# A sequence FFT, a maxout layer and a SoLU layer on one core: the first batch's first transform in f32, its input laid out by loads, other fillers and other priorities

## The chip, the cores and the metric

The kernel runs on one core of one Trainium2 chip. The time is the device time of one execution in microseconds, from three runs of the kernel before, and one more execution that the hardware profiler recorded. TensorE (PE) multiplies matrices and loads weights beside that (PEld), VectorE (DVE), ScalarE (ACT) and GpSimd (POOL) do the rest, and SyncE (SP) issues all DMA transfers on one queue.

## The reference

```python
X = np.fft.fft(x, axis=1)                 # x: 8 batches x 3072 rows x 256, f32
X = np.fft.fft(X, axis=2)
x = X.real.reshape(8 * 3072, 256)
h = np.maximum(np.maximum(x @ w1, x @ w2), x @ w3)      # 256 -> 768
x = h @ w_out                                           # 768 -> 256
h = x @ w_in                                            # 256 -> 1024
e = np.exp(h - h.max(-1)); sm = e / (e.sum(-1) + 1e-9)
solu = h * sm
ln = (solu - mean(solu)) / sqrt(var(solu) + 1e-6) * g_ln
out = ln @ w_out2                                       # 1024 -> 256
```

## The kernel before

Products that need the accuracy of f32 are done in f16 with a high and a low part of each factor: ScalarE makes the high part (`split_hi`, L367), VectorE or GpSimd the low part (`split_lo`, L370), and TensorE adds three products (`TERMS`: high by high, high by low, low by high).

**The transforms.** The transform over the 256 columns is folded into the weights of layer 1: TensorE multiplies them with a table of cosines (cw) in f32 (L996, L1003, L1101). The transform over 3072 rows has two steps. A batch of x is loaded in four chunks c (`x_load`, L409, tile xs); VectorE (batch 0) or GpSimd (the others) folds each with its mirror image (L416, L458, tile uv). The sum of squares over the batch gives a scale, a power of two (L425 to L441, tile xb). x is split into f16 parts with that scale (`x_hi`, `x_lo`, tile uh: in batch 0 straight from uv by L367 and L370). **alpha** (`alpha_mm`, L496, L499) multiplies it with the table cal; ScalarE casts the high part out (L527, tile x) and VectorE the low part (L531). `last_mm` does one row that stands alone. SP transposes the result (tile z), and **beta** (L555, table cb) is the second step; its parts are pq.

**The layers.** A batch gives 6 blocks of 512 rows, 48 in all. In each block layer 1 (L660, tile l, weights wl and w3l; L681, L701 and L702 put the two halves of a product together in sv, L707 takes the maximum), its second product (m, L726, tile rhl as input), then h (L790), the SoLU and the norm on VectorE, ScalarE and GpSimd, and the last product (omm, L865) follow each other. TensorE does 12 groups of l, 6 of m, 4 of h and 4 of omm in a block.

**The weights** arrive as 64-bit numbers. `from_f64` loads the two words (L951, tile raw), ScalarE takes the exponent (L963) and VectorE puts an f32 together with three instructions (L967, L968, L970). The raw words of w_out and w_out2 share the buffers xs and uv with x. Subtraction (L990), folding, a bound of the largest element (am, spread, L390), a scale (sc) and the split into wl, wo, win, w3l and wf follow, all before or between the first blocks.

**The order.** The program is written by a list scheduler in Python (`Schedule`). Each operation has an engine, a duration, a due time `vt` (in blocks) plus a number from the table `BIAS`, dependences and buffers that it takes and gives back (`CAPACITY`). On each engine the ready operation with the earliest start, and among those with the smallest due time, comes next. So `BIAS` sets the order of instructions on every engine. Where the plan leaves TensorE idle before the first h, `keep_warm` puts matmuls of zeros (L1315, tile spare from zz) into the gap.

Of the kernel before, what the change touches and what calls it, by code (L numbers as in the profile page):

```python
# [1361 lines left out]
```

## Time and profile before

| | us |
|---|---|
| median of 3 runs | 1998.37 (1997.97 to 1999.53) |
| profiled execution | 2002.85 |
| its span, first to last instruction | 2001.1 |
| TensorE busy in the span | 1975.3 |
| VectorE busy in the span | 1696.1 |

The granted TensorE clock is 0.997 of full speed in the mean. A row of the timeline or of the costliest groups names the line, the engine, the operation, and the output and inputs by their names in the program; a bracket gives the idle time of the engine ahead of it and what ended it. An f32 matmul leaves two records in the trace, so 16 records of such a line are 8 matmuls. In the profiled execution layer 1 starts at 78 us and h at 118 us after the first instruction. What comes before is loading, decoding and folding weights and batch 0's transforms.

### The profile page before, as it was taken

The numbers are of one execution on the slowest core, as the hardware profiler recorded it, in microseconds if no ns is written. First come the engines' busy times: TensorE is split into PE (matmuls) and PEld (weight loads), VectorE is DVE, ScalarE is ACT, GpSimd is POOL, SyncE is SP. The second block draws the span as 40 slices with busy tenths as digits, with TensorE's granted clock in tenths as the row PEclk, the third lists the DMA queues.
The fourth block names the chain that finished last, engine by engine and source line by source line (L and its number), as shares of the span: only waits on it lengthen the run. The fifth ranks groups of instructions, "written<-read, shape, count | busy, mean of one in ns | idle before, by whom it ended". The sixth has DMA issues, their size and how long they took to land.

```text
span 2001.1 us, 40923 instructions
## 1 busy us (share of the span) xinstructions
PE 1975.3 (99%) x15041; PEld 1348.0 (67%) x15041; DVE 1696.1 (85%) x3886; ACT 1493.0 (75%) x2929; POOL 1315.2 (66%) x1395
## 2 busy tenths in 40 slices
PE   8899999999999999999999999999999999999998
PEld 4556666766666666766677666666667666666666
DVE  7888889888888888888888888888888888888885
ACT  5778888876787677877778767787677766776775
POOL 0389997955588556976569656765556665655653
PEclk9999999999999999999999999999999999999999
DMA  8424754633444334443434444333343333333334
GB/s 282 96 51 103 136 119 78 130 80 70 85 89 113 72 82 75 110 91 76 80 75 106 80 80 80 65 75 80 70 85 70 76 73 75 75 76 63 75 78 103
DMA packets 471819, 178.81 MB, mean 89 GB/s; under 512 B 452697, under 2 KB 452922, under 8 KB 468410
## 3 DMA queue, kind: packets, MB, share of 16 engines
q1 hardware_dynamic: 471618, 176.20, 42.1%
q8 instruction: 117, 1.92, 0.4%
q14 instruction: 84, 0.69, 0.1%
HBM read 37.75 MB, written 25.17 MB: 31 GB/s over the span
## 4 chain that ended last, share of the span: by engine, by line
PE 82%; DVE 6%; POOL 5%; ACT 3%; DMA 3%; issue 2%; SPq 0%; POOLq 0%; DVEq 0%; ACTq 0%
PE omm L865 22%; PE h L790 21%; PE l L660 19%; PE m L726 16%; PE beta L555 2%; PE alpha L496 1%; POOL uv L458 1%; DMA xs<-in_x_dram 1%; DVE l L681 1%; POOL xs L416 1%; POOL vh L851 1%; POOL rhl L716 1%; DMA vt<-vh 1%; ACT jk L825 1%; POOL mo L741 1%
## 5 line engine op out<-in xcount | busy, mean ns | idle before, releaser
L865 PE MATMUL omm<-wf,vt 128*128 128x256 f16 x4608 | 533.4, 273 | 2.8 <-ACT ob L872 1.7
L790 PE MATMUL h<-win,mo 128*128 128x512 f16 x2280 | 523.4, 379 | 1.6 <-DVE v L820 1.3
L716 POOL TENSOR_TENSOR rhl<-sv,rhl 128x512 f16<-128x512 f32 x288 | 334.4, 1162 | 269.5 <-ACT rhl L711 255.6
L865 PEld LDWEIGHTS <-vt 128*128 128x128 f16 x4608 | 450.3, 98 | 75.3 <-issue 1.9
L660 PE MATMUL l<-pq,wl 128*128 128x256 f16 (+2 forms) x3456 | 445.2, 272 | 7.2 <-DVE sv L707 3.1
L851 POOL TENSOR_TENSOR vh<-v,vh 128x1024 f16<-128x1024 f32 x188 | 400.8, 2132 | 75.8 <-ACT vh L847 62.7
L681 DVE SCALAR_TENSOR_TENSOR l<-ny,wn,l 128x256 f32<-128x256 f32 (+1 forms) x672 | 317.6, 483 | 155.1 <-ACT bs L367 141.9
L726 PE MATMUL m<-rhl,wo 128*128 128x512 f16 x1728 | 414.8, 379 | 0.1
L660 PEld LDWEIGHTS <-wl 128*128 128x128 f16 x3456 | 330.9, 97 | 108.0 <-DVE sv L702 11.9
L790 PEld LDWEIGHTS <-mo 128*128 128x128 f16 x2304 | 223.6, 98 | 240.6 <-DVE v L820 4.6
L367 ACT ACTIVATE bs<-l 128x256 f32<-128x256 f32 x560 | 206.1, 380 | 153.7 <-PE l L660 120.2
L825 ACT ACTIVATE jk<-v,hst 128x1024 f16<-128x1024 f32 x192 | 220.4, 1148 | 73.5 <-DVE v L820 72.4
L799 DVE TENSOR_REDUCE hst<-h 128x1 f32<-128x1024 f32 x190 | 231.7, 1219 | 50.7 <-PE h L790 49.7
L726 PEld LDWEIGHTS <-wo 128*128 128x128 f16 x1728 | 163.9, 98 | 153.0 <-issue 0.4
L820 DVE SCALAR_TENSOR_TENSOR v<-h,hst,e 128x1024 f32<-128x1024 f32 x190 | 243.2, 1280 | 23.7 <-ACT e L814 17.5
L814 ACT ACTIVATE e<-h,hst,xb 128x1024 f32<-128x1024 f32 x190 | 228.9, 1205 | 6.3
L711 ACT CAST rhl<-sv 128x512 f16<-128x512 f32 x288 | 176.0, 613 | 73.3 <-DVE sv L707 38.4
L707 DVE SCALAR_TENSOR_TENSOR sv<-l,sv 128x512 f32<-128x512 f32 x288 | 197.8, 687 | 3.6
L847 ACT CAST vh<-v 128x1024 f16<-128x1024 f32 x192 | 199.6, 1039 | 0.9 <-DMA vt<-vh 0.9
L838 POOL TENSOR_SCALAR hst<-hst,sc 128x1 f32<-128x1 f32 x192 | 66.2, 345 | 136.3 <-ACT jk L825 111.4
L741 POOL TENSOR_TENSOR mo<-s,mw 128x512 f16<-128x512 f32 x96 | 121.0, 1276 | 27.3 <-ACT mw L367 21.8
L872 ACT ACTIVATE ob<-omm,hst 128x256 f32<-128x256 f32 x192 | 89.9, 469 | 57.6 <-PE omm L865 42.1
(167 smaller groups left out, 2323.3 us busy)
## 6 DMA issues: line engine op xcount, KB each, us to landing
xs<-in_x_dram SPq DMA_DIRECT2D x32, 768.0 KB, 6.3
out_dram<-ob SPq DMA_DIRECT2D x96, 256.0 KB, 2.2
raw<-in_w_dram SPq DMA_DIRECT2D x4, 768.0 KB
vt<-vh SPq DMA_TRANSPOSE x192, 4.3
xs<-in_w_out_dram SPq DMA_DIRECT2D x8, 256.0 KB, 6.2
raw<-in_w_in_dram SPq DMA_DIRECT2D x4, 512.0 KB, 4.0
cb<-in_c_beta_dram SPq DMA_DIRECT2D x1, 1553.0 KB, 8.8
x<-in_w_dram SPq DMA_DIRECT2D x2, 768.0 KB
```

Source lines behind the costliest of these rows:

```text
L367: act.activation(dst, src, AF.Copy, scale=scale)
L660: mm(o, w_[w], hl[:, a, e, c0:c0 + n_], start=(n == 0), stop=(n == 2))
L681: dve.scalar_tensor_tensor(p[:, 0:WA], pq[s][1][:, 0:WA], w, p[:, 0:WA], ALU.mult, ALU.add)
L716: pool.tensor_tensor(t[:, 1], svs.pop((s, j, 0)), t[:, 0], ALU.subtract)
L726: mm(m[:, h], wo[:, w, j, hs], t[:, a], start=(j == 0 and n == 0), stop=(j == NJF - 1 and n == 2))
L790: mm(hp[:, f], m[:, a, d, ts_], win[:, w, d, fs], start=(n == 0), stop=(n == 5))
L799: dve.tensor_reduce(st[:, 0], y["h"], op=ALU.max, axis=AX.XY, negate=True)
L814: act.activation(y["e"], y["h"], AF.Exp, bias=st[:, 11], scale=xbt[s // NSB][:, 12:13], accum_out=st[:, 3])
L820: dve.scalar_tensor_tensor(y["v"], y["h"], st[:, 2], y["e"], ALU.mult, ALU.mult, accum_out=st[:, 4])
L825: act.activation(new(hpool[0], "jk", [128, 2, 512], F16), y["v"], AF.Square, bias=st[:, 4], scale=-float(FF2), accum_out=st[:, 6])
L851: engine.tensor_tensor(y["vh"][:, 1], y["v"].rearrange("p a b -> p (a b)"), y["vh"][:, 0], ALU.subtract)
L865: mm(y["o"][:, 0:D], vt[:, a * 8 + c], wf[:, w, c], start=(n == 0), stop=(n == 23))
```

## The change

1. In batch 0, `x_hi` and `x_lo` are gone. Alpha multiplies uv itself, in f32, with a new f32 table calf; x's scale is put on that table by one ScalarE instruction (`cals`). 33 matmuls stand for 99, and `last_mm` has 2 for 4. The buffer uv is given back by alpha.
2. x lies in memory in the order of its loads, so that the 8 KiB of a row of a chunk, and the rows of a chunk, follow each other; before, the rows of a chunk were 32 KiB apart.
3. calf is loaded after x, cal later than before. The table of ones is gone, and the factor 1/1024 of the mean of w_out2's rows is applied where the mean is copied out of PSUM. zz has 256 columns in place of 512.
4. `keep_warm` fills a gap wholly, with matmuls of 256 columns, where it filled three quarters with matmuls of 512: 377 of them in place of 149, of which 154 in a row at the start.
5. `BIAS` has new numbers, within 60 blocks in place of some 2000, and own keys for blocks 0 to 2. The plan's durations of a few loads change.

With these the order of nearly every engine changes. On SP, cw was the first load, and now it follows the first two chunks of x.

```diff
-BIAS = {("xla", 0): -534.137, ("xgh", 0): 286.232, ("xfly", 0): -6.751, ("xsq", 0): 385.004, ("xhi", 0): 285.602,
...
+BIAS = {("xla", 0): -20.556, ("xgh", 0): 23.969, ("xfly", 0): -58.75, ("xsq", 0): -12.676, ("al", 0): 23.231, ("ah",
...
+    full = out.reshape(NA * NJ + 1, 3 * 2 * NQ * NJ) * 16.0
...
+    return table, np.ascontiguousarray(np.concatenate([full, last], axis=1).astype(np.float32))
...
+    calf = wp.tile([97, c_first.shape[1]], F32, name="calf")
...
-        sp.dma_start(t[0:96], x[b, :, c * GC:(c + 1) * GC])
+        sp.dma_start(t[0:96], x[b, c])
...
     def alpha_mm(b, c, h):
...
-        u = xuh[b, c]
+        u = xuh[b, c] if b else xuv[b, c]
...
         for g in range(GC):
             n, kind = (97, 1 + h) if c == 0 and g == 0 else (96, 0)
+            if b == 0:
+                mm(p[:, g * 96:(g + 1) * 96], u[0:n, h, g], calf[0:n, kind * 96:(kind + 1) * 96])
+                continue
             for i, (a, w) in enumerate(TERMS):
                 mm(p[:, g * 96:(g + 1) * 96], u[0:n, a, h, g], table(kind, w, n), start=(i == 0), stop=(i == 2))
-        if c == 0 and h == 1:
+        if c == 0 and h == 1 and b == 0:
+            mm(p[0:1, 0:96].rearrange("p (q j) -> p q j", j=2)[:, :, 0], u[:, 1, 0, 0:1],
+               calf[:, 96:192].rearrange("p (q j) -> p q j", j=2)[:, :, 0])
+        elif c == 0 and h == 1:
...
     def last_mm(b):
...
+            if b == 0:
+                mm(p[0:1, o:o + n], calf[:, 3 * 96:3 * 96 + 1], xuv[b, 0][:, h, 0, 0:n])
+                continue
...
-        op(("xla", *k), "SP", 3500 if b else 2600, x_load, k, v - 0.5, deps=[("xla", b, c - 1)] if c else [("xla", b - 1, NCH - 1)] * (b > 0) + [("open",), ("gd", "f", 1)] * (b == 1),
+        op(("xla", *k), "SP", 3500 if b else 2200, x_load, k, v - 0.5, deps=[("xla", b, c - 1)] if c else [("xla", b - 1, NCH - 1)] * (b > 0) + [("open",), ("gd", "f", 1)] * (b == 1),
...
+        if b == 0:
+            return
         v += 0.2
-        normed = b > 0
-        if normed:
-            op(("xnm", *k), "ACT", 1040, x_norm, k, v, deps=[("xsc", b)])
...
-                op(("al", *kh), "PE", 520, alpha_mm, kh, v + 0.04 * h, deps=[("xlo", b, c), ("cal",)] + [("al", b, 0, 0)] * (not first) + [("al", b, c, 0)] * h,
+                op(("al", *kh), "PE", 520 if b else 760, alpha_mm, kh, v + 0.04 * h,
+                   deps=[("xlo", b, c) if b else ("xfly", b, c), ("cal",) if b else ("cals",)] + [("al", b, 0, 0)] * (not first) + [("al", b, c, 0)] * h,
+    def const_load5():
+        sp.dma_start(calf[0:96], c_first[0:96])
+        sp.dma_start(calf[96:97], c_first[96:97])
...
-    zz = wp.tile([128, 512], F16, name="zz")
+    zz = wp.tile([128, 256], F16, name="zz")
...
-    ones = wp.tile([128, 128], F32, name="ones")
-    pool.memset(ones, 1.0 / FF2)
...
-    op(("cal",), "SP", 900, const_load, (), -0.85, lag=2000)
+    op(("calf",), "SP", 900, const_load5, (), -0.85, lag=2000)
+    op(("cals",), "ACT", 360, lambda: split_hi(calf, calf, xbt[0][0:97, 11:12]), (), -0.85, deps=[("calf",), ("xsc", 0)])
+    op(("cal",), "SP", 900, const_load, (), -0.25, lag=2000)
...
-        put(("ld", *key), "SP", 3.4 * n, f64_load, (key, srcs, n, home), v - 0.2, deps=after, take=[home] * first + [*take], lag=1900)
+        put(("ld", *key), "SP", 3.0 * n, f64_load, (key, srcs, n, home), v - 0.2, deps=after, take=[home] * first + [*take], lag=1900)
...
-            mm(p[:, 0:D], ones, w2_rows(c), start=(c == 0), stop=(c == 7))
+            mm(p[:, 0:D], unit, w2_rows(c), start=(c == 0), stop=(c == 7))
...
-        act.copy(mean, tmp.pop("mean")[:, 0:D])
+        split_hi(mean, tmp.pop("mean")[:, 0:D], 1.0 / FF2)
...
-        n = int(gap * 0.75 / 216)
+        n = int(gap / 109 + 0.5)
...
-            mm(p[:, 0] if tag == "h" else p, zz[:, 0:128], zz)
+            mm(p[:, 0, 0:256] if tag == "h" else p[:, 0:256], zz[:, 0:128], zz)
...
-        "x": np.stack([xs[:, n[:96]][..., X_PAIRS], xs[:, m[:96]][..., X_MIRROR]], axis=3),
+        "x": np.stack([xs[:, n[:96]][..., X_PAIRS], xs[:, m[:96]][..., X_MIRROR]], axis=3).reshape(
+            B, 96, NCH, GC, 2, D).transpose(0, 2, 1, 3, 4, 5),
```

Three places show how the order moves. The first is VectorE around the first casts of alpha. xb is x's scale, L967, L968 and L970 are the decode (of a half of w_out2 on uv, of the layer-1 weights on st), L370 on uh the low parts of x, L531 alpha's low parts. Before:

```order
L440 TENSOR_SCALAR xb<-xb 128x1
L967 TENSOR_SCALAR uv<-uv 128x1024
L441 RECIPROCAL xb<-xb 128x1
L968 SCALAR_TENSOR_TENSOR uv<-xs,uv 128x1024
L970 SCALAR_TENSOR_TENSOR uv<-xs,uv 128x1024
L370 SCALAR_TENSOR_TENSOR uh<-uv,xb,uh 97x1024
L370 SCALAR_TENSOR_TENSOR uh<-uv,xb,uh 96x1024
L531 TENSOR_TENSOR x_355<-alpha,x_355 128x6x16x4 x2
L967 TENSOR_SCALAR st<-st 128x768
L968 SCALAR_TENSOR_TENSOR st<-raw,st 128x768
```

And now, with the same lines under new numbers (L454 and L455 the scale, L989, L990 and L992 the decode, L548 alpha's low parts):

```order
L454 TENSOR_SCALAR xb<-xb 128x1
L455 RECIPROCAL xb<-xb 128x1
L989 TENSOR_SCALAR uv<-uv 128x1024
L990 SCALAR_TENSOR_TENSOR uv<-xs,uv 128x1024
L548 TENSOR_TENSOR x_452<-alpha,x_452 128x6x16x4 x2
L989 TENSOR_SCALAR st<-st 128x768
L992 SCALAR_TENSOR_TENSOR uv<-xs,uv 128x1024
L990 SCALAR_TENSOR_TENSOR st<-raw,st 128x768
L548 TENSOR_TENSOR x_452<-alpha,x_452 128x6x16x4
```

The low parts of x are gone, and alpha's low parts stand ahead of the last step of the decode on uv.

The second place is VectorE around the low parts of the layer-1 weights (wl), after their scale sc. am and spread lead to the scale of the third product's weights, et is the row that stands alone. Before:

```order
L1027 RECIPROCAL sc<-am 128x1
L1034 TENSOR_SCALAR wn<-wn,sc 128x12
L370 SCALAR_TENSOR_TENSOR wl_74<-st,sc,wl_74 128x768 x4
L531 TENSOR_TENSOR x_355<-alpha,x_355 128x6x16x4 x4
L390 TENSOR_REDUCE am<-spread 128x2
L361 TENSOR_SCALAR am<-am 128x2
L364 TENSOR_SCALAR am<-am 128x2
L1027 RECIPROCAL sc<-am 128x1 x2
```

And now:

```order
L1049 RECIPROCAL sc<-am 128x1
L1056 TENSOR_SCALAR wn<-wn,sc 128x12
L548 TENSOR_TENSOR x_452<-alpha,x_452 128x6x16x4
L535 TENSOR_TENSOR et<-last,et 1x129
L384 SCALAR_TENSOR_TENSOR wl_75<-st,sc,wl_75 128x768 x4
L989 TENSOR_SCALAR uv<-uv 128x1024
L990 SCALAR_TENSOR_TENSOR uv<-xs,uv 128x1024
L1141 TENSOR_REDUCE am<-w3f 128x1
L992 SCALAR_TENSOR_TENSOR uv<-xs,uv 128x1024
L384 SCALAR_TENSOR_TENSOR pq<-beta,pq 128x256 x2
L989 TENSOR_SCALAR st<-st 128x512
L404 TENSOR_REDUCE am<-spread 128x2
```

All of alpha's low parts of batch 0 now come ahead of wl, and the decode of the other half of w_out2 on uv stands between wl and the next scale.

The third place is TensorE at alpha's first matmuls. prep is the fold of the layer-1 weights st with cw. Before:

```order
L1003 MATMUL prep<-cw,st 128x1 x6
L1315 LDWEIGHTS zz
L1315 MATMUL spare<-zz 128x512
L996 MATMUL prep<-st,cw 128x384 x8
L496 LDWEIGHTS uh
L496 MATMUL alpha<-cal,uh 128x96
```

And now:

```order
L1018 MATMUL prep<-st,cw 128x384 x4
L504 MATMUL alpha<-calf,uv 128x96 x8
L509 MATMUL alpha<-calf,uv 1x48
L1018 MATMUL prep<-st,cw 128x384 x4
L504 MATMUL alpha<-calf,uv 128x96 x8
```

Four of the eight matmuls of this part of the fold have moved behind alpha's first nine.

## Rows read from the trace of the kernel before

**Rows 1.** The page's head and part 1: busy us, share, instructions.

```profile
span 2001.1 us, 40923 instructions
PE 1975.3 (99%) x15041; PEld 1348.0 (67%) x15041; DVE 1696.1 (85%) x3886; ACT 1493.0 (75%) x2929; POOL 1315.2 (66%) x1395
```

**Rows 2.** Stretches: length, busy us by engine, granted clock, DMA share, GB/s.

```profile
0.00:79.00 79.00, 68.74 (x388) 42.05 (x389) 60.79 (x98) 48.08 (x91) 9.17 (x16) 0.94 0.69 208
79.00:118.00 39.00, 34.48 (x237) 20.07 (x236) 34.71 (x91) 31.04 (x65) 21.90 (x17) 0.96 0.28 64
118.00:200.00 82.00, 78.39 (x594) 50.70 (x593) 71.86 (x174) 64.85 (x128) 77.47 (x70) 1.00 0.43 94
...
200.00:1900.00 1700.00, 1697.81 (x13145) 1168.81 (x13143) 1460.03 (x3381) 1282.04 (x2527) 1157.05 (x1229) 1.00 0.42 84
1900.00:2001.00 101.00, 95.85 (x687) 66.33 (x684) 68.76 (x145) 67.00 (x123) 49.58 (x66) 1.00 0.43 89
```

**Rows 3.** The same for L1315 alone (fillers; PE, PEld, clock).

```profile
0.00:200.00 200.00, 40.51 (x149) 15.31 (x149) 0.97 0.50 133
```

**Rows 4.** Timeline of PE: start, us, engine, line, operation, tiles, records.

```profile
78.11 1.76 PE L660 MATMUL l<-pq,wl 128*128 128x256 f16 x12
...
118.37 2.89 PE L790 MATMUL h<-win,mo 128*128 128x512 f16 x12
...
122.61 2.75 PE L726 MATMUL m<-rhl,wo 128*128 128x512 f16 x12
```

**Rows 5.** Timeline of DVE; the bracket is the wait ahead.

```profile
6.65 0.56 DVE L967 TENSOR_SCALAR st<-st 128x768 int32<-128x768 int32 x1 [6.65 <-ACT st L963]
...
22.57 1.22 DVE L416 TENSOR_TENSOR xs<-xs 96x1024 f32<-96x1024 f32 x1 [0.50 <-DMA xs<-in_x_dram]
...
29.45 1.22 DVE L416 TENSOR_TENSOR xs<-xs 96x1024 f32<-96x1024 f32 x1 [1.25 <-DMA xs<-in_x_dram]
...
46.72 0.56 DVE L531 TENSOR_TENSOR x<-alpha,x 128x384 f16<-128x384 f32 x1 [4.09 <-ACT x L527]
...
69.55 1.07 DVE L531 TENSOR_TENSOR x<-alpha,x 128x384 f16<-128x384 f32 x2 [0.81 <-ACT x L527]
71.42 0.42 DVE L390 TENSOR_REDUCE am<-spread 128x2 f32<-128x256 f32 x1 [0.80 <-PE spread L386]
...
76.97 0.42 DVE L370 SCALAR_TENSOR_TENSOR pq<-beta,pq 128x256 f16<-128x256 f32 x1 [1.37 <-ACT pq L367]
```

**Rows 6.** Costliest groups, first 110 us: count, busy us, mean ns, idle before.

```profile
L370 DVE SCALAR_TENSOR_TENSOR uh<-uv,xb,uh 96x1024 f16<-96x1024 f32 x3 | 3.7, 1275 | 0.0
...
L370 DVE SCALAR_TENSOR_TENSOR uh<-uv,xb,uh 97x1024 f16<-97x1024 f32 x1 | 1.3, 1277 | 0.0
```

**Rows 7.** The page's part 6, DMA issues: KB each, us to landing.

```profile
xs<-in_x_dram SPq DMA_DIRECT2D x32, 768.0 KB, 6.3
...
raw<-in_w_in_dram SPq DMA_DIRECT2D x4, 512.0 KB, 4.0
cb<-in_c_beta_dram SPq DMA_DIRECT2D x1, 1553.0 KB, 8.8
```

**Rows 8.** Timeline of PE from 38 to 59 us.

```profile
38.02 7.64 PE L996 MATMUL prep<-st,cw 128*128 128x384 f32 x16
45.49 1.19 PE L496 MATMUL alpha<-cal,uh 97*128 97x96 f16 x24
...
50.94 1.40 PE L1003 MATMUL prep<-cw,st 128*128 128x1 f32 x12
...
53.25 5.70 PE L1101 MATMUL prep<-st 128*128 128x256 f32 x24 [0.38 <-ACT wn L1010]
```

**Rows 9.** Stretches of 10 us, columns as in rows 2.

```profile
40.00:50.00 10.00, 9.82 (x67) 5.85 (x66) 5.47 (x8) 6.83 (x13) 0.00 (x0) 0.87 0.51 187
50.00:60.00 10.00, 9.56 (x60) 7.38 (x58) 9.89 (x17) 9.90 (x23) 0.82 (x1) 1.00 0.34 107
```

**Rows 10.** Waits over the span: who, for whom, us, count, longest.

```profile
PEld L660 <- DVE sv L702: 14.2, 30, 2.6
```

More of the change, by code (lines that the diff above doesn't have):

```diff
@@ new lines @@
+BIAS = {("xla", 0): -20.556, ("xgh", 0): 23.969, ("xfly", 0): -58.75, ("xsq", 0): -12.676, ("al", 0): 23.231, ("ah",
+        0): -60, ("alo", 0): -52.601, ("et", 0): 29.373, ("eth", 0): -43.075, ("etl", 0): 10.283, ("xall", 0): 23.881,
+        ("xsc", 0): -26.16, ("mu", 0): 11.757, "me": 59.365, ("xla", 1): -18.328, ("xgh", 1): 60, ("xfly", 1): 1.452,
+        ("xsq", 1): -37.532, ("xnm", 1): 60, ("xhi", 1): 59.384, ("xlo", 1): 48.774, ("al", 1): 8.556, ("ah", 1):
+        55.39, ("alo", 1): 31.069, ("et", 1): -60, ("eth", 1): -43.856, ("etl", 1): 18.251, ("xall", 1): -51.191,
+        ("xsc", 1): 39.983, ("mu", 1): 59.947, "xla": 17.835, "xgh": 60, "xfly": 28.075, "xsq": 57.869, "xnm": 53.6,
+        "xhi": 49.146, "xlo": -60, "al": -57.232, "ah": -36.37, "alo": -52.597, "et": 29.3, "eth": 58.676, "etl":
[21 rows of a table added]
+        14.258, ("sub", 1): 58.839, ("wc", 1): -3.382, ("wce", 1): 26.182, ("am", 1): -16.392, ("wcn", 1): -48.51,
+        ("wne", 1): -60, ("wz", 1): -15.067, ("sub", 2): 26.595, ("wc", 2): 60, ("wce", 2): -0.157, ("am", 2): 10.639,
+        ("wcn", 2): -60, ("wne", 2): -59.88, ("wz", 2): 25.16, ("amj",): -29.398, ("ws", "dg"): -46.767, ("ws",
+        "all"): -25.27, ("ws", "pow"): 12.54, ("wsc", "part"): 59.106, ("wsc",): -60, ("whi", 1): 60, ("wlo", 1): 60,
[5 rows of a table added]
+        ("os3", "dg"): -60, ("os3", "all"): -59.998, ("os3", "pow"): -50.608, ("scm", "part"): -42.972, ("scm",):
+        -3.929, ("w3r",): -60, ("onm", 0): 43.578, ("ohi", 0): -33.397, ("olo", 0): -56.914, ("onm", 1): 60, ("ohi",
+        1): 59.968, ("olo", 1): -60, ("w3h",): 59.51, ("w3l",): 59.628, ("ld", "i"): 52.041, ("ga", "i"): 6.024,
+        ("gd", "i"): -59.474, ("ami", 0): 15.611, ("wio", 0): -25.491, ("wih", 0): 40.398, ("wil", 0): -21.222,
+        ("ami", 1): 47.997, ("wio", 1): -13.282, ("wih", 1): 56.262, ("wil", 1): -52.215, ("amij",): 12.268, ("is",
+        "dg"): 32.279, ("is", "all"): -21.105, ("is", "pow"): 15.883, ("isc",): -52.766, ("win",): -47.198, ("gl",):
+        50.125, ("ld", "f"): 32.894, ("ga", "f"): -57.815, ("gd", "f"): 28.936, ("wfg", 0): 57.981, ("wfg", 1):
+        44.531, ("wfg", 2): -60, ("wfg", 3): 60, ("wfm",): 11.484, ("wfe",): 30.935, ("wfs", 0): -49.479, ("amf", 0):
+        41.77, ("wfs", 1): 51.353, ("amf", 1): 15.768, ("amfj",): -60, ("fs", "dg"): 5.292, ("fs", "all"): -35.17,
+        ("fs", "pow"): -60, ("wfc", "part"): 2.909, ("wfc",): 36.713, ("wfn", 0): 60, ("wfh", 0): 49.376, ("wfl", 0):
+        44.453, ("wfn", 1): -50.807, ("wfh", 1): 6.062, ("wfl", 1): -60, ("wf",): -58.537, ("open",): 45.016, "cal":
[3 rows of a table added]
+        1): 52.792, ("rh", 2): 59.879, ("rlo", 0): 6.505, ("rlo", 1): -6.361, ("rlo", 2): -38.418, ("m", 0): -5.203,
[11 rows of a table added]
+        -29.789, ("xsq", 2): -60, ("xnm", 2): 46.34, ("xhi", 2): -59.706, ("xlo", 2): -13.134, ("al", 2): -10.446,
+        ("ah", 2): 59.223, ("alo", 2): -12.222, ("et", 2): -57.377, ("eth", 2): -5.423, ("etl", 2): -31.449, ("xall",
+        2): -23.734, ("xsc", 2): -60, ("mu", 2): -4.586, ("me", 2): -32.3, ("calf",): 45.0, ("cals",): -52.246}
@@ L162, in _alpha @@
     last[24:48] = 16.0
-    return np.ascontiguousarray(np.concatenate([w.transpose(0, 2, 1, 3).reshape(NA * NJ + 1, -1), last], axis=1))
+    table = np.ascontiguousarray(np.concatenate([w.transpose(0, 2, 1, 3).reshape(NA * NJ + 1, -1), last], axis=1))
+    return table, np.ascontiguousarray(np.concatenate([full, last], axis=1).astype(np.float32))
 def _beta():
@@ L320, in fft_moe_solu_kernel @@
 @with_exitstack
-def fft_moe_solu_kernel(ctx, tc, x, x_last, w1, w2, w3, w_out, w_in2, w_out2, g_ln, c_alpha, c_beta, c_w, c_eye, out):
+def fft_moe_solu_kernel(ctx, tc, x, x_last, w1, w2, w3, w_out, w_in2, w_out2, g_ln, c_alpha, c_first, c_beta, c_w, c_eye, out):
     nc = tc.nc
@@ L465, in x_norm, with x_hi, x_lo @@
         split_hi(xuv[b, c], xuv[b, c], x_unit(b, c))
[L467 removed]
+    def x_hi(b, c):
         t = new(fp, "uh", [97, 2, 2, GC, 128], F16)[0:x_rows(c)]
[L469 to L472 removed]
+        act.copy(t[:, 0], xuv[b, c])
         xuh[b, c] = t
[L475 removed]
+    def x_lo(b, c):
         t = xuh[b, c]
[L477 to L480 removed]
+        pool.tensor_tensor(t[:, 1], xuv.pop((b, c)), t[:, 0], ALU.subtract)
     TERMS = ((0, 0), (0, 1), (1, 0))
@@ L616, in fft_moe_solu_kernel @@
                 first = c == 0 and h == 0
-                op(("al", *kh), "PE", 520, alpha_mm, kh, v + 0.04 * h, deps=[("xlo", b, c), ("cal",)] + [("al", b, 0, 0)] * (not first) + [("al", b, c, 0)] * h,
-                   take=["misc", "x1"] if first else ["misc"], give=[("uh", ("xhi", b, c))] if h and c else [])
+                op(("al", *kh), "PE", 520 if b else 760, alpha_mm, kh, v + 0.04 * h,
+                   deps=[("xlo", b, c) if b else ("xfly", b, c), ("cal",) if b else ("cals",)] + [("al", b, 0, 0)] * (not first) + [("al", b, c, 0)] * h,
+                   take=["misc", "x1"] if first else ["misc"],
+                   give=[] if not h else ([("uh", ("xhi", b, c))] if c else []) if b else [("uv", ("xfly", b, c))] * (c > 0))
                 op(("ah", *kh), "ACT", 380, alpha_hi, kh, v + 0.04 * h, deps=[("al", *kh)])
                 op(("alo", *kh), "DVE", 470, alpha_lo, kh, v + 0.04 * h, deps=[("ah", *kh)], give=[("misc", ("al", *kh))])
-        op(("et", b), "PE", 300, last_mm, (b,), v, deps=[("al", b, 0, 1)], take=["misc", "et"], give=[("uh", ("xhi", b, 0))])
+        op(("et", b), "PE", 300, last_mm, (b,), v, deps=[("al", b, 0, 1)], take=["misc", "et"], give=[("uh", ("xhi", b, 0)) if b else ("uv", ("xfly", b, 0))])
         op(("eth", b), "ACT", 120, last_hi, (b,), v, deps=[("et", b)])
@@ L1321, in fft_moe_solu_kernel @@
     sch.run()
-_INS = ["x", "x_last", "w1", "w2", "w3", "w_out", "w_in2", "w_out2", "g_ln", "c_alpha", "c_beta", "c_w", "c_eye"]
+_INS = ["x", "x_last", "w1", "w2", "w3", "w_out", "w_in2", "w_out2", "g_ln", "c_alpha", "c_first", "c_beta", "c_w", "c_eye"]
 def kernel(**inputs):
```

46 lines of the change are left out of this document (6 added, 40 removed), and 69 rows, old and new, of the table BIAS.

## The prediction

> **What bounds the kernel now.** I read the busy shares first. One core runs for a span of 2001.1 us and TensorE is busy for 1975.3 us of it, 99%; VectorE follows with 85% [rows 1]. An average over the whole span hides stages, so next I read busy time by stretch [rows 2]. From 200 to 1900 us TensorE is busy for 1697.81 of 1700 us at clock 1.00: there it is the bound, and only less TensorE work, or a wait that opens again in every block, can move the time. In the last 101 us it is idle for 5.15 us. In the first 200 us it is busy for 68.74 + 34.48 + 78.39 = 181.61 us, so it idles for 18.4 us.
>
> Busy is not the same as useful there. The filler matmuls of line 1315 take 40.51 us of those 200 [rows 3]. Real work thus loses 18.4 + 40.5 = 58.9 us at the start, and whatever brings the first real matmuls forward moves the end by as much, because behind it TensorE never waits. The landmarks are the first layer-1 matmul at 78.11 us and the first matmul of h at 118.37 us [rows 4].
>
> Who holds up the start? VectorE is busy for 60.79 of the first 79 us and for 34.71 of the next 39 [rows 2]. Its order of time with the wait ahead of each instruction gives the rest [rows 5]: 6.65 us for the first weights, 0.50 + 1.25 = 1.75 us for x to land, 4.09 us for the cast of batch 0's first transform (alpha), and 0.81 + 0.80 + 1.37 = 2.98 us around the second transform (beta) and the weight scale. So the start is VectorE's queue plus a few holes, and each term below is asked for what it takes out of that queue or those holes.
>
> **The change part by part.** All terms are against the profiled execution's 2002.85 us (the span and 1.75 us around it), which is 4.48 us above the median of 1998.37; I take a difference in the one as a difference in the other.
>
> 1. The low parts of batch 0's x go: four VectorE instructions, three together 3.7 us and one of 1.3 us [rows 6]. They stand in VectorE's queue ahead of the first layer-1 matmul, in the new order nothing of their kind takes their places (the first order fence), and VectorE has little idle time there. If all of it reaches the end, −5.0; if the time only fills with waits, 0. I take −5.0, since VectorE's busy share is the nearest row. The high parts leave ScalarE too; with 48 of 79 us busy it has room [rows 2], so I count that at nothing, as ScalarE's own idle time hides it already.
>
> 2. The loads of x become contiguous. Four loads of 768 KB take 6.3 us each to land. The raw parts of w_in, 512 KB, take 4.0 us, and the beta table, 1553 KB, takes 8.8 us [rows 7]. A line through those two gives (8.8 − 4.0) / (1553 − 512) = 4.6 ns per KB, so 768 KB would take 4.0 + 256 × 0.0046 = 5.2 us: x is 1.1 us late per load. That can only be won where VectorE waits for x, 1.75 us in all. Bounds 0 and −1.75; I take half, −0.9, as one load's 1.1 us lies between the two waits of 0.50 and 1.25. On the queue itself (SP), cw moves from the first place to behind two chunks of x, so the fold of the weights begins later; fillers stand there, and term 6 carries it.
>
> The row above shows x slower than its neighbours by bytes. The Trainium skill, page "DMA: Bandwidth & Descriptors", section "Latency and other measured facts", says that HBM rows a large power of two apart slow a copy down (it gives 207 GB/s at a 512 KiB pitch and 103 at 4 MiB) and that laying tiles out contiguously restores the rate. Its pitches begin far above the 32 KiB of x here, and no run of it stands in this trace; by that rule the whole 1.75 us would go, and the sum below would be 0.85 us lower.
>
> 3. The wait of 4.09 us for alpha's first cast [rows 5]. Behind the last low part, VectorE waited while TensorE did eight f32 matmuls of the weight fold, from 38.02 to about 45.5 us, and only then alpha [rows 8]. In the new order alpha needs no low part, and half of that fold (four of eight matmuls) stands ahead of alpha's first nine (the third order fence). Against that it needs a new ScalarE instruction, the scaling of calf, queued between x's scale and alpha; what waits behind it on ScalarE is one exponent step of the weights. Bounds 0 and −4.1; I take half, −2.0.
>
> 4. The holes of 2.98 us around beta [rows 5]. In the new order the decode of the second half of w_out2 (L989, L990, L992 on uv) stands between the weight lows and that scale (the second order fence), where the old one has only alpha's lows; it fills holes with work that is due anyway. Bounds 0 and −3.0; I take half, −1.5.
>
> 5. The clock. The granted clock is 0.87 from 40 to 50 us and 1.00 from 50 to 60 [rows 9]. Eight f32 matmuls of 384 columns took 7.64 us in the first stretch, twelve of 256, as many columns, 5.70 in the second [rows 8]: 1.9 us lost to the lower of the two levels. Longer runs of fillers ahead of them may keep the clock. Bounds 0 and −1.9; I take −1.0.
>
> 6. Alpha in f32, and more filler. 33 matmuls in f32 replace 99 in f16. Those ran 24 in 1.19 us, 0.050 each, so 4.9 us. For f32 at 96 columns there is no row; the neighbours are one column, six matmuls (two records each) in 1.40 us, 0.23 each, and 256 columns, twelve in 5.70 us, 0.475 each [rows 8]. That bounds the 33 at 7.7 to 15.7 us, so +2.8 to +10.8 of TensorE time, in a stretch where TensorE has fillers to spare. Only what lies between x's scale and the first casts is on the path. I take +1.5 there, near the one-column row's half, and keep 0 to +10.8. The fillers become 377 of 256 columns in place of 149 of 512. At 2.75/12 = 0.229 us for 512 columns [rows 4], and half that for 256, they are 43.2 in place of 34.1 us: +9.1 us. Where a gap of the planner's is real they cost nothing, as TensorE waits there anyway; where what it waits for comes early, they are in the way. The first run alone is 154, some 17.6 us, with the fold of the weights behind it. Bounds 0 and +9.1; I take a third, +3.0.
>
> 7. The steady part. All priorities change, so do those of 40 blocks in which TensorE has 2.19 us of idle time in 1700 [rows 2]. There is nothing to gain there beyond those 2.2 us, and an order can only be worse: bounds −2.2 and about +11 (rival 2). I take 0, the nearer row. The same for the last 101 us, with at most 5.15 us to win. The mean's scale in its eviction, the dropped table of ones and calf's load (0.1 MB) are off VectorE's queue: 0.
>
> Sum: −5.0 − 0.9 − 2.0 − 1.5 − 1.0 + 1.5 + 3.0 = −5.9. The profiled execution would be 1997.0 us and the median 1998.4 − 5.9 = 1992.5 us.
>
> **The rivals.**
>
> Rival 1, no change. The work taken out of VectorE's queue ahead of the first layer-1 matmul comes back between it and the first h: part of the weights' decode now stands later, VectorE is busy for 34.71 of those 39 us, and h waits for VectorE's additions and lows whatever came before. Against it: the 5.0 us of lows are gone for good, not moved. If terms 3, 4 and 5 bring nothing and filler takes 3.0, the sum is −5.0 − 0.9 + 1.5 + 3.0 = −1.4: about 1997.
>
> Rival 2, slower. The new priorities make TensorE's weight loads of layer 1 (L660) wait for VectorE's joining of a product's two halves (L702) in every other block, a place where the trace shows a wait already: 14.2 us over 30 waits, 0.47 us each [rows 10]. One more such wait in 24 of the 48 blocks costs 11.3 us, and with the start's −5.9 the sum is +5.4: 2003.8 us. It decides from (5.9 + 4.0) / 48 = 0.21 us per block on. For it: the order is wholly new there, and VectorE is busy for 1460 of those 1700 us. Against it: buffers and dependences of a block are as before, and the reserve of 14% is the same.
>
> Rival 3, a large gain. Every lower bound is met: −5.0 − 1.75 − 4.1 − 3.0 − 1.9 with filler and f32 at 0 to +3.0 is −16 to −13: about 1984. Against it: VectorE's queue has no room for it, as 95.5 of the first 118 us are busy and only 5.0 of that is removed.
>
> **How the numbers follow.** Two measurements of this kernel can be told apart from about 0.2%, 4.0 us: faster is below 1994.4, slower above 2002.4. I give the forecast 0.55, rival 1 0.25, rival 2 0.13, rival 3 0.07. The forecast's own range is 1986 to 1996, from terms 3 to 6 taken to either side; a tenth of it lies within 0.2%. Faster is then 0.9 × 0.55 + 0.07 = 0.57 (rounded up), the same 0.1 × 0.55 + 0.25 = 0.30 (rounded down), and slower rival 2's 0.13. The range is 1983.5 to 2002.5: it holds the forecast, rival 1 and most of rival 3, and leaves out most of rival 2.
>
> **What would show it.** Right: no low parts of batch 0 on VectorE, alpha's first lows not behind a wait of 4 us, the first layer-1 matmul at about 70 us, the first h at about 112, and a stretch from 200 us on as full as before. Term 2: x landing in about 5 us. Term 5: a clock of 1.00 between 25 and 60 us. Term 6: f32 alpha matmuls of 0.23 to 0.3 us, and VectorE or ScalarE not waiting for a TensorE that runs fillers. The forecast is wrong if the first h is not earlier although the first layer-1 matmul is (rival 1), if idle time or waits for VectorE appear between 200 and 1900 us (rival 2), or if the first h comes before 108 us (rival 3).

## The result, and the profile after

The changed kernel takes 2008.8 us (median of 4 runs, 2004.43 to 2013.19) against 1998.17 for the kernel before: a ratio of 1.0054, with a 95% interval of 1.0042 to 1.0067. It is slower by some 10 us where 5.9 us less were forecast. Its profiled execution took 2010.87 us, 8.0 more than that of before.

First the page's head and busy times of the kernel after, with columns as in [rows 1]:

```profile
span 2009.1 us, 41243 instructions
PE 1984.6 (99%) x15236; PEld 1372.4 (68%) x15236; DVE 1696.1 (84%) x3882; ACT 1485.8 (74%) x2926; POOL 1312.1 (65%) x1394
```

Busy shares tell nothing here: TensorE is at 99% in both. The stretches of [rows 2] do, for the kernel after:

```profile
0.00:79.00 79.00, 73.66 (x511) 60.10 (x512) 56.12 (x91) 42.73 (x86) 3.04 (x13) 0.96 0.76 221
79.00:118.00 39.00, 38.85 (x326) 28.91 (x326) 35.84 (x101) 34.74 (x72) 31.87 (x23) 1.00 0.11 27
...
200.00:1900.00 1700.00, 1689.35 (x13073) 1159.38 (x13071) 1459.59 (x3373) 1266.51 (x2504) 1146.12 (x1213) 1.00 0.40 82
```

TensorE's idle time between 200 and 1900 us, 2.19 us before, is 10.65 now, where nothing was expected to change. The start, by contrast, did in this profile what was forecast. The timeline of TensorE after, with the rows that answer to [rows 4]:

```profile
70.75 1.48 PE L678 MATMUL l<-pq,wl 128*128 128x256 f16 x12
...
112.06 2.75 PE L808 MATMUL h<-win,mo 128*128 128x512 f16 x12
```

The first layer-1 matmul comes 7.4 us earlier and the first h 6.3 us earlier (forecast: about 70 and 112).

To see where time goes while TensorE looks busy, I kept a ledger. Each TensorE matmul of real work has a price, the usual distance between the starts of two such matmuls (0.1085 us for 256 columns and 0.216 for 512, from the steady part of before; the others likewise; fillers cost nothing). Both kernels hold 1908.0 us of work by these prices, and what elapsed beyond it is lost time. Alpha's 33 f32 matmuls of batch 0 are thus booked like the 99 that they replace; the distances of their starts add up to some 3 us more, which stand in the lost time of the start. For the profiled executions, in us:

```
                                        0 to 200   200 to 1950   1950 to end   span
before                                      66.8          20.5           5.8   2001.1
after                                       61.4          33.0           6.7   2009.1
all edits, order of before                  66.0          20.8           7.6   2002.4
fillers alone, order of before              64.9          19.8           7.2   1999.9
all edits, order of before, 3/4 filled      64.0          22.6           8.3   2002.9
after, with the old layout of x             55.4          33.3           6.6   2003.3
after, 3/4 filled                           59.2          39.3           6.6   2013.1
after until block 2, then before's order    62.8          22.2           6.3   1999.3
before until block 2, then after's order    72.9          27.7           5.8   2014.4
```

After against before: −5.4 at the start, +12.5 in the middle, +0.9 at the end, together +8.0. The part on which the forecast spent six of its seven terms came out within 0.5 us, and the term that it set at zero cost 12.5. Each row is one execution, and these lay between 2.7 us below and 4.7 us above the medians of their kernels (before: 4.7 above), so a few us between two rows of the start say little. The middle is clearer: 19.8 to 22.6 us in the five rows whose blocks follow the old order, 27.7 to 39.3 in the four with the new one.

Where in the middle? The longest waits of TensorE after, from 200 to 1950 us (who, for whom, us, count, longest):

```profile
PEld L808 <- DVE v L838: 12.0, 25, 1.4
PEld L678 <- DVE sv L720: 6.4, 11, 2.1
PE h L808 <- DVE v L838: 4.7, 13, 1.1
PE l L678 <- DVE sv L720: 2.8, 3, 1.8
```

And the same view of the kernel before:

```profile
PEld L660 <- DVE sv L702: 6.3, 20, 0.5
PEld L790 <- DVE v L820: 2.4, 8, 0.4
```

h waits for v (L838, L820 before), the VectorE instruction that reads h last and so frees its PSUM, the memory that TensorE writes. Between a layer-1 matmul and an h behind it the ledger loses 8.3 us after and 1.6 before, more than half of the 12.5; most of the rest lies before layer 1 (behind m, omm and h: +1.6, +2.0, +1.1). h is done in four tiles a block. At 20 tiles the loss before h is over 0.12 us in both of two profiles with this order (of 21 and 20 such tiles), and 14 of the 21 are the second tile of a block, 5 the third. One of the second tiles, VectorE in the kernel after, from the reduction of a block's first tile to its v:

```profile
859.62 1.21 DVE L817 TENSOR_REDUCE hst<-h 128x1 f32<-128x1024 f32 x1
861.30 0.88 DVE L699 SCALAR_TENSOR_TENSOR l<-ny,wn,l 128x256 f32<-128x256 f32 x2 [0.47 <-ACT bs L381]
862.09 0.42 DVE L719 SCALAR_TENSOR_TENSOR sv<-l,bs 128x256 f32<-128x256 f32 x1
862.43 0.41 DVE L720 SCALAR_TENSOR_TENSOR sv<-l,bs 128x256 f32<-128x256 f32 x1
862.76 0.42 DVE L719 SCALAR_TENSOR_TENSOR l<-l,bs 128x256 f32<-128x256 f32 x1
863.21 0.43 DVE L720 SCALAR_TENSOR_TENSOR l<-l,bs 128x256 f32<-128x256 f32 x1
863.55 0.20 DVE L820 TENSOR_SCALAR hst<-hst,xb 128x1 f32<-128x1 f32 x1
863.68 0.69 DVE L725 SCALAR_TENSOR_TENSOR sv<-l,sv 128x512 f32<-128x512 f32 x1
...
864.83 1.28 DVE L838 SCALAR_TENSOR_TENSOR v<-h,hst,e 128x1024 f32<-128x1024 f32 x1
```

ScalarE's exponential and TensorE's next h at the same place:

```profile
861.76 1.20 ACT L832 ACTIVATE e<-h,hst,xb 128x1024 f32<-128x1024 f32 x1
...
866.18 2.76 PE L808 MATMUL h<-win,mo 128*128 128x512 f16 x12 [0.27 <-DVE v L838]
```

The exponential ends at 862.96 us, but v starts at 864.83: between the reduction and v stand two whole products of layer 1 and their maximum (L725), and the last of these are done only behind the exponential. The same tile in the kernel before:

```profile
847.27 1.23 DVE L799 TENSOR_REDUCE hst<-h 128x1 f32<-128x1024 f32 x1 [1.77 <-PE h L790]
848.41 0.48 DVE L681 SCALAR_TENSOR_TENSOR l<-ny,wn,l 128x256 f32<-128x256 f32 x1
848.80 0.21 DVE L802 TENSOR_SCALAR hst<-hst,xb 128x1 f32<-128x1 f32 x1
849.00 0.42 DVE L701 SCALAR_TENSOR_TENSOR sv<-l,bs 128x256 f32<-128x256 f32 x1
849.34 0.42 DVE L702 SCALAR_TENSOR_TENSOR sv<-l,bs 128x256 f32<-128x256 f32 x1
...
850.19 1.28 DVE L820 SCALAR_TENSOR_TENSOR v<-h,hst,e 128x1024 f32<-128x1024 f32 x1
```

Here one product stands ahead of v, and its exponential ended at 850.06, 0.13 us before v. Over the tiles between 200 and 1900 us, v starts 0.59 us behind its exponential before and 1.38 after. VectorE is busy for 1460 us of these 1700 in both.

### The profile page after: what moved, and what is told of

Its sections match the earlier page's. It is cut to its first block, busy times and chain, and to the rows that moved or that the text cites. A ratio compares the mean times of both kernels' runs of the same rounds, so it can differ in the third digit from the quotient of the medians.

```text
span 2009.1 us, 41243 instructions
## 1 busy us (share of the span) xinstructions
PE 1984.6 (99%) x15236; PEld 1372.4 (68%) x15236; DVE 1696.1 (84%) x3882; ACT 1485.8 (74%) x2926; POOL 1312.1 (65%) x1394
## 5 line engine op out<-in xcount | busy, mean ns | idle before, releaser
L817 DVE TENSOR_REDUCE hst<-h 128x1 f32<-128x1024 f32 x190 | 231.4, 1218 | 61.4 <-PE h L808 60.6
L838 DVE SCALAR_TENSOR_TENSOR v<-h,hst,e 128x1024 f32<-128x1024 f32 x190 | 243.2, 1280 | 31.5 <-ACT e L832 22.2
L725 DVE SCALAR_TENSOR_TENSOR sv<-l,sv 128x512 f32<-128x512 f32 x288 | 197.2, 685 | 2.4
```

Of the source, the lines that this page charges most:

```text
L817: dve.tensor_reduce(st[:, 0], y["h"], op=ALU.max, axis=AX.XY, negate=True)
L838: dve.scalar_tensor_tensor(y["v"], y["h"], st[:, 2], y["e"], ALU.mult, ALU.mult, accum_out=st[:, 4])
```

## The experiments

In nine of the twelve an order was given to the scheduler as a list in place of the priorities, so that an edit and an order can be told apart; where an experiment names an order, every engine follows it but for what is said. The other three (gaps of the changed kernel filled to three quarters, the old layout of x, fillers alone) keep the scheduler. The time is the median, the ratio is to the kernel before, measured beside each run.

**All edits, order of before.** The low and high parts are left out of the old order, and calf, its scaling and cal are put in; `todo` is that order.

```diff
-                rank = (max(start, clock[e] + WINDOW[e]), o.vt)
...
+            for n, k in enumerate(todo):
...
```

> All edits of the change (f32 alpha with calf, contiguous x, whole-gap fillers, unit for ones), but every engine keeps the order of the kernel before: the low and high parts of x in batch 0 are left out of it, calf is loaded where cal was, cals follows x's scale, cal follows the beta table. Theory A (the new order of the blocks from 200 us on costs about 12 us, at VectorE's v, which frees h's PSUM; the edits gain at the start): 1992 to 1997 us, and TensorE's waits for v between 200 and 1900 us at about 3 us as before. Rival B (an edit costs it: the f32 alpha or more filler or the new loads): 2001 us or more, although the order is the old one.

Measured: 2003.81 us, ratio to before 1.0025 (1.0017 to 1.0034). The time lies in rival B's range (2001 us or more) and not in theory A's, though the waits for v are back at 2.7 us, as theory A has it. So neither holds alone: of the changed kernel's 10 us half is gone with the order, but the edits alone do not gain, they cost. VectorE's timeline at the start shows why the missing low parts bring so little in the old order:

```profile
44.59 0.56 DVE L803 TENSOR_TENSOR x<-alpha,x 128x384 f16<-128x384 f32 x1 [3.89 <-ACT x L799]
...
58.24 0.29 DVE L659 TENSOR_REDUCE am<-spread 128x1 f32<-128x128 f32 x1 [2.66 <-PE spread L655]
```

The wait for alpha's cast is as long as before [rows 5], since the fold still stands ahead of alpha on TensorE, and a wait for the weight scale is new. The first h is at 117.30 us, 1.1 us earlier than before.

**The changed kernel, v one operation earlier** at 117 places. The instruction just ahead of v goes behind it; in the tile shown above that is the maximum:

```diff
-L725 SCALAR_TENSOR_TENSOR sv<-l,sv
 L838 SCALAR_TENSOR_TENSOR v<-h,hst,e
+L725 SCALAR_TENSOR_TENSOR sv<-l,sv
```

> The changed kernel, with one thing moved: in blocks 3 to 44, in 117 of 168 places, the VectorE operation that stood just ahead of v (SCALAR_TENSOR_TENSOR v<-h,hst,e) now follows it; nothing moves on the other engines. Theory A: TensorE's waits for v (L808 in all 17 us) fall to under 8 us and the time from 2008.8 to 1999 to 2004 us. Rival C (VectorE is simply full, and what is pushed behind v makes layer 1 wait instead): waits for sv rise by as much and the time stays within 3 us of the changed kernel's. Rival B (edits): no change.

Measured: 2045.95 us, 1.0232 (1.0219 to 1.0245). Theory A's remedy fails: 37 us slower than the changed kernel. Rival C has the direction, but it wanted at most 3 us. The waits, 200 to 1950 us (L931 is layer 1, L1061 is h; "issue" is time in which the profile shows nothing that was waited for):

```profile
PEld L931 <- issue: 32.8, 49, 1.7
PEld L931 <- DVE sv L973: 22.0, 32, 2.3
PE l L931 <- DVE sv L978: 20.4, 32, 1.5
...
PEld L1061 <- DVE v L1091: 6.4, 12, 1.2
```

The waits for v fall from 16.7 to 9.6 us (3.2 of it on PE itself), and layer 1 now waits far more for what was pushed back.

**The changed kernel, gaps filled to three quarters.**

```diff
-        n = int(gap / 109 + 0.5)
+        n = 2 * int(gap * 0.75 / 216)
```

> The changed kernel with the gaps filled to three quarters as before (258 fillers of 256 columns in place of 377); order and all else unchanged. Theory A: the fillers are not what costs: within 3 us of the changed kernel, its landmarks before 200 us moved by less than 3 us. Rival B (whole-gap filler delays the chain at the start): faster by 4 us or more, first h earlier. If fillers hold the clock up, as the forecast's term 5 has it, this one shows lower clocks in the first 60 us and is up to 3 us slower.

Measured: 2013.23 us, 1.0077 (1.0063 to 1.0090), 4.4 us above the changed kernel. Fewer fillers are not faster. The mean clock was 0.997 in all six runs, while the changed kernel's runs had 0.997 to 1.000. Its profile has the first h at 109.52 us, earlier than after, but loses 39.3 us in the middle with the same instructions.

**The changed kernel with the old layout of x.**

```diff
-        sp.dma_start(t[0:96], x[b, c])
+        sp.dma_start(t[0:96], x[b, :, c * GC:(c + 1) * GC])
...
```

> The changed kernel with x in memory as before (rows of a chunk 32 KiB apart); order and all else unchanged. The forecast's term 2: 0 to 2 us slower, x landing about 1 us later per load in batch 0 (waits of VectorE for x in the first 40 us longer by as much). Rival: the loads are held by the shared DMA engines, not by the rows' distance, and nothing changes (within 0.5 us at the start). Theory A expects nothing of it between 200 and 1900 us.

Measured: 2007.84 us, 1.0047 (1.0033 to 1.0060): no difference from the changed kernel. An 8 KiB packet of batch 0 takes 0.545 us before, 0.550 after and 0.529 here in the mean. No effect of the layout shows.

**The changed kernel until the first h of block 8, then the order of before.** In this kernel and the later ones with two orders, the list is the one order up to a point and the other's remaining operations behind it.

> The changed kernel with its own order up to the first h of block 8 (about 400 us) and from there on the order of the kernel before; some 30 rows of VectorE between the two are neither. Theory A2: the order of the later blocks is what costs. From 400 to 1950 us the changed kernel loses 29.9 us of TensorE time, the kernel before 16.8; with the old order there, 13 us come back: 1993 to 1999 us, and the loss from 500 to 1900 us is within 2 us of the kernel before's. Rival D: the old order is only good behind its own start, and work that comes earlier loses the time later whatever the order: 2003 us or more.

Measured: 2012.11 us, 1.0069 (1.0054 to 1.0085). The time speaks for rival D, but the ledger shows a stall of the splice: 19.5 us are lost between 400 and 500 us, one wait of 14 us among them, and from 500 to 1950 us 16.2 us, against 15.6 in the kernel before and 28.3 after. By the time alone this settles nothing; the splice at a better place follows below.

**Fillers alone.** The kernel before with the new rule of fillers.

```diff
-        n = int(gap * 0.75 / 216)
+        n = int(gap / 109 + 0.5)
...
+            mm(p[:, 0, 0:256] if tag == "h" else p[:, 0:256], zz[:, 0:128], zz)
...
```

> The kernel before with one edit: the gaps filled wholly with matmuls of 256 columns; order and all else unchanged. The run with all edits in the old order was 4.5 us slower than the kernel before although its clock stood at 1.00. Theory F (filler in the way of real work, at a higher clock): 2000.5 to 2005 us, clock 1.00 in the first 110 us. Rival G (the f32 alpha costs it, the filler nothing): within 1.5 us of the kernel before or faster.

Measured: 2003.29 us, 1.0016 (1.0007 to 1.0026), in theory F's range. The clock from 30 to 50 us, which had been 0.79 and 0.87, is held (stretches of 10 us):

```profile
30.00:40.00 10.00, 10.00 (x57) 7.16 (x57) 9.93 (x17) 7.57 (x13) 0.73 (x1) 1.00 1.03 385
40.00:50.00 10.00, 10.00 (x98) 7.72 (x97) 8.31 (x12) 8.90 (x18) 0.00 (x0) 1.00 0.60 207
```

In the old order the whole-gap filler costs some 3 us net, although the clock is higher.

**All edits, order of before, gaps filled to three quarters.**

> All edits in the old order as in the run before with that order, but the gaps filled to three quarters (matmuls of 256 columns). Theory F: without the whole-gap filler the f32 alpha shows what it is worth: 1994 to 1999 us. Rival G (the f32 alpha costs): 2002 us or more. The low parts taken out of VectorE should show as the first h about 3 to 5 us earlier than in the kernel before, at the same clock, if the forecast's first term was right.

Measured: 2006.24 us, 1.0030 (1.0021 to 1.0040): rival G, and against theory F. The first h is at 114.62 us, 3.75 earlier than before, as term 1 wanted, at a higher clock than before in that stretch; but the time is not better. Eight of nine runs had a mean clock of 0.996 or 0.997, most runs of before 0.998 or 0.999. Why the edits cost in the old order is not settled.

**The changed kernel until block 2, then the order of before.** At about 155 us both orders have done the same operations but for a few, so this splice joins smoothly.

> The changed kernel with its own order only until block 2 (about 155 us), where both orders have done the same work but for a few operations, and the order of the kernel before from there on; the splice at block 8 had one stall of its own of some 14 us. From the first h to the end the old order took 1883 to 1888 us in four profiles, the new one 1897 to 1904 in three. Theory A2: 106 to 112 us to the first h, then 1883 to 1890: 1991 to 2002 us, best guess 1996, and a loss of TensorE time from 200 to 1950 us of 20 to 23 us in place of 33. Rival D (an earlier start is lost again whatever the order): 2003 us or more, with the loss after 200 us at 28 or more.

Measured: 1997.68 us against 2001.16 for the kernel before beside it, 0.9986 (0.9977 to 0.9995): faster than both kernels, by 2.8 us than before. With the same edits but the old order at the start too, the ratio was 1.0025, so what is gained needs the start's new order. The middle loses 22.2 us in place of 33.0, and TensorE is busy again:

```profile
200.00:1900.00 1700.00, 1696.13 (x13132) 1167.52 (x13130) 1459.46 (x3381) 1278.67 (x2520) 1155.10 (x1226) 1.00 0.41 84
```

**The kernel before until block 2, then the order of after.** No edit at all.

> The kernel before with no edit but the order: its own until block 2, the changed kernel's from there on. Theory A2: the later order costs 12 us or more without any of the edits: 2009 to 2016 us, with TensorE waiting for v some 17 us between 200 and 1950 us. Rival D: the old start's lateness hides the waits, and it is within 4 us of the kernel before.

Measured: 2011.72 us, 1.0050 (1.0036 to 1.0063): the whole loss of the changed kernel, with none of its edits. Its waits for v, 200 to 1950 us (L1043 is h):

```profile
PEld L1043 <- DVE v L1073: 11.3, 26, 1.1
PE h L1043 <- DVE v L1073: 3.7, 13, 0.8
```

The loss from 200 to 1950 us is 27.7 us, 7.2 above before's, 5.9 of it between layer 1 and h; another 6 us are lost at the splice, between 175 and 200 us. So the later order brings its waits into a start that never had them, but how much of the 10.6 us is the order and how much the splice is only known from the one profile.

**The smooth splice with gaps filled to three quarters.**

> The run before that starts new and goes on in the old order, with gaps filled to three quarters (matmuls of 256 columns). If whole-gap fillers stand in the way by more than the clock they hold is worth, 1 to 4 us faster than with whole gaps; if the clock is worth more, 1 to 4 us slower at a clock of 0.997.

Measured: 2001.3 us, 1.0000 (0.9991 to 1.0009). With the new start the whole gaps are worth 0.14% by the ratios, 2.8 us (3.6 by the medians). Eight of ten runs here had a mean clock of 0.997 or less; ten of the eleven with whole gaps had 0.999 or 1.000.

**The maximum behind the first v** in 25 blocks of the changed kernel.

> The changed kernel; in 25 of the blocks 3 to 44 the maximum of a block three further on (L725), which stood on VectorE between the reduction and v of a block's first tile, now follows v; the other engines keep their order (ScalarE but for three instructions). In the changed kernel TensorE loses 8.3 us between a layer-1 matmul and the next h (200 to 1950 us; 1.6 in the kernel before), nearly all at the same 20 tiles in two profiles, 17 of them a block's second tile, which waits for the first one's v. Theory V (this maximum ahead of v is what delays it): that loss falls to 4 us or less and the time by 3 to 6 us, to 2003 to 2006 us. Rival C (the order has no room, the maximum is as urgent for layer 1): losses before layer 1 rise by as much or more, and the time stays at 2007 us or rises.

Measured: 2026.83 us, 1.0144 (1.0130 to 1.0158), 18 us slower than the changed kernel. The loss between layer 1 and h falls from 8.3 to 5.0 us; between m and layer 1 it rises from 1.8 to 13.1 and within layer 1 from 4.9 to 13.8. The waits, 200 to 1950 us (L932 is layer 1, L1062 is h):

```profile
PEld L932 <- issue: 23.8, 29, 1.9
PE l L932 <- DVE sv L979: 17.2, 21, 1.7
PEld L932 <- DVE sv L974: 12.5, 13, 2.1
PEld L1062 <- DVE v L1092: 8.0, 17, 1.4
```

**h one operation later** on TensorE, for the second tile of 42 blocks of the changed kernel.

> The changed kernel; in blocks 3 to 44 the h of a block's second tile follows the TensorE operation that stood behind it (a layer-1 product in 37, the second product of layer 1 in 3, beta in 2); no other engine's order changes. Theory V (only the place of h against v is wrong, by a few tenths of a us): the loss between layer 1 and h falls to 4 us or less, and the time by 3 to 6 us. Rival C: the operation put ahead of h waits itself for VectorE (its PSUM is freed by the same queue), and the time stays within 2 us of the changed kernel's or rises.

Measured: 2069.41 us, 1.0353 (1.0339 to 1.0368). The loss between layer 1 and h falls from 8.3 to 5.9, within layer 1 it rises from 4.9 to 52.8. Theory V falls with both of these, for the time, and rival C stands. At the second tiles themselves the loss before h does fall, from 5.6 us in the changed kernel to 1.9 with the maximum moved and 1.0 with h moved, so what stood there did hold h up; but more is lost elsewhere (at the third tiles 2.5 becomes 3.3 and 6.0, and layer 1 loses what is said above). The reading that fits: in the new order v, which frees h's PSUM, and the joining and maximum, which free layer 1's, are due at the same time on VectorE, and neither can be late. Moving one of them did not repair the order in any of three ways. Since every engine's order changes in the kernel after and in both splices, no run shows how much VectorE's order costs by itself.

## Why the prediction was wrong, point by point

**Step 7, the steady part: this is the step that failed.** It took 0, with bounds of −2.2 and +11, as "the nearer row", which was the 2.19 us of idle time that the old order had; and its opening part had counted on it, "because behind it TensorE never waits". It measured +12.5 in the profiles, outside the bounds. In its place the runs show waits that the new order opens behind the start. Three runs show it: the old order from block 2 on takes the changed kernel's ratio from 1.0054 to 0.9986, the new order from there on adds 10.6 us to the kernel before (some of it at the splice), and the edits in the old order leave the middle at 20.8 us. Rival 2 had the mechanism's kind, its price (+11.3) and its sign, but in the main the wrong place: weight loads of layer 1 waited 7.7 us for L702's counterpart (L720) over the whole span, less than before [rows 10], while the waits for v grew and the loss before h with them; some 5 of the 12.5 us do lie before layer 1. It had 0.13. What was there to be read: VectorE was busy for 1460 of 1700 us, every block's PSUM is freed by it, and the step said itself that "an order can only be worse", yet put nothing into the sum for it.

**Terms 1 to 6, the start**, −5.9 forecast, −5.4 measured at 200 us. That the sum came within 0.5 us is luck: not each term held, and the changed kernel with the old layout of x, which has the same order and fillers, lost 55.4 us at the start in its profile in place of 61.4. Two estimates from the medians give less: the +10.6 less the 12.5 and 0.9 of the profiles leave −2.8 for the start, and the smooth splice, −2.8 in all with +1.7 and +0.5 behind 200 us, leaves −5.0. Term by term:
- Term 1 (low parts, −5.0): not a time of its own. In the old order VectorE waited instead: still 3.89 us for alpha, which came 2.1 us earlier because the fold ahead of it took 5.33 us at a clock of 1.00 in place of 7.64, and 2.66 us for the spread where the other two low parts had stood. The first h was 1.1 us earlier; 3.75 us with fewer fillers.
- Term 2 (x, −0.9): wrong. Waits for x in VectorE's timeline after, in place of 1.75 us:

```profile
12.89 1.23 DVE L430 TENSOR_TENSOR xs<-xs 97x1024 f32<-97x1024 f32 x1 [0.47 <-DMA xs<-in_x_last_dram]
...
27.13 1.22 DVE L430 TENSOR_TENSOR xs<-xs 96x1024 f32<-96x1024 f32 x1 [0.53 <-DMA xs<-in_x_dram]
...
34.62 1.22 DVE L430 TENSOR_TENSOR xs<-xs 96x1024 f32<-96x1024 f32 x1 [1.97 <-DMA xs<-in_x_dram]
```

  They are 2.97 us, and 1.34 with the old layout. x's packets are as long in either layout. The 6.3 us of [rows 7] was the median of all 32 loads of x: in batch 0 the three landings on record took 8.2, 8.8 and 9.3 us, so the line through two other transfers was no measure of them. The rule of the Trainium skill, page "DMA: Bandwidth & Descriptors", section "Latency and other measured facts", on row pitches of a large power of two does not show at 32 KiB.
- Term 3 (alpha's first wait, −2.0): measured −1.8, as 1.74 and 0.51 us replace 4.09:

```profile
46.66 0.56 DVE L548 TENSOR_TENSOR x<-alpha,x 128x384 f16<-128x384 f32 x1 [1.74 <-ACT x L544]
47.73 0.56 DVE L548 TENSOR_TENSOR x<-alpha,x 128x384 f16<-128x384 f32 x1 [0.51 <-ACT x L544]
```

- Term 4 (the holes around beta, −1.5): of the 2.98 us, one wait of 1.08 is left, for alpha's last cast, and 0.30 for an exponent is new ahead of the first layer-1 matmul, −1.6. VectorE no longer waits for the spread or for beta's parts there.

```profile
60.52 0.56 DVE L548 TENSOR_TENSOR x<-alpha,x 128x384 f16<-128x384 f32 x1 [1.08 <-ACT x L544]
...
65.62 0.69 DVE L989 TENSOR_SCALAR uv<-uv 128x1024 int32<-128x1024 int32 x1 [0.30 <-ACT uv L985]
```

- Term 5 (the clock, −1.0): nothing of it in the profile after. The granted clock was 0.90 from 30 to 40 us and 0.76 from 40 to 50 (before: 0.79 and 0.87), and the fold's four matmuls ahead of alpha took 2.15 us more than the four behind it:

```profile
40.25 5.00 PE L1018 MATMUL prep<-st,cw 128*128 128x384 f32 x8
...
47.12 2.85 PE L1018 MATMUL prep<-st,cw 128*128 128x384 f32 x8
```

  With the old layout of x, at 1.00, the first four took 2.75, and the first h came at 105.66 us, below the 108 that was to speak for rival 3. So two profiles of this order lie 6.4 us apart at the first h, more than the term's whole range; 1.6 us of that are the shorter waits for x.
- Term 6 (alpha in f32 +1.5, filler +3.0): the f32 alpha took 0.24 us per matmul, next to the one-column row, and all 33 about 8.2 us (bounds 7.7 to 15.7). The first eight, and the fillers of the first 200 us:

```profile
45.09 1.92 PE L504 MATMUL alpha<-calf,uv 97*128 97x96 f32 x16
```

```profile
0.00:200.00 200.00, 48.97 (x377) 38.17 (x377) 0.98 0.57 143
```

  The fillers grew by 8.5 us (9.1 worked out). Their net worth depends on the order: +3 us alone in the old one, −3 to −4 us with the new start.

**From the profile to the median.** The forecast takes a difference of profiles as one of medians; the first came out as +8.0 and the second as +10.6. The profiled execution of before lay 4.7 us above its median and that of after 2.1 above its own, so this step alone was off by 2.6 us.

## What to carry to other kernels

Where an engine is full, the wait it does not show still has a price: before a new order is put through forty blocks, look at the engine that frees its buffers and at how many instructions stand between two of its deadlines in the old order, and give the steady part a term in the sum, not the idle time of the old order. When a change mixes edits with a new order, run the edits in the old order and the old program in the new order; here that split a loss of 10 us into a start worth keeping and a steady part worth undoing. A wait that shrinks where its cause is moved, and grows elsewhere, need not have been misread: here two deadlines met on one engine, although it was idle for 14% of the time.

## What was not expected of the hardware

Runs of one program spread with the mean clock: after took 2004.43 and 2006.74 us at 1.000, 2010.87 at 0.998 and 2013.19 at 0.997. Even the first two lie above all four runs of before beside them (at most 1999.53), so the clock is not what made the change slower. In the profile after, the clock was 0.90 from 30 to 40 us and 0.76 from 40 to 50, with two idle stretches of TensorE of 1.01 and 1.47 us between 30 and 40; in the profile with the old layout of x, with the same order and fillers, it was 1.00 in each of the first eleven stretches of 10 us, and the first h came at 105.66 us in place of 112.06. What makes the one or the other happen was not tried.

The three experiments on the order's details cost 18 to 61 us for one instruction moved in 25 to 117 places, while the wholly different order costs 12 in the middle. Why small moves cost more than the large one was not tried.
